# Attention followed by a two-layer gelu network on one NeuronCore: reordering attention against layer 2, and narrower filler matmuls

## The chip, the cores and the metric

The kernel runs on one core of a Trainium2 chip. A core has five engines that each work through their own instruction list: TensorE (PE in the profile, with its weight loads as PEld), VectorE (DVE), ScalarE (ACT), GpSimd (POOL) and SyncE (SP), which here only issues transfers. They meet through semaphores. The metric is the device time of one execution in microseconds; the figure that counts is the median over runs.

## The reference

Inputs are q, k and v of shape (8, 8, 576, 64): 8 batches, 8 heads, 576 tokens, 64 values per head. A third input s (8, 8, 576) makes a decay bias. For each batch and head:

```
scores = (q @ k.T) / 8
cum    = cumsum(max(s, 0))
bias   = -(cum[i] - cum[j])
scores = where(j > i, -1e9, scores + min(bias, 0))
attn   = exp(scores - max);  attn = attn / (sum(attn) + 1e-9)
out    = attn @ v
```

The heads of a token are put side by side, which gives x with 8 * 576 = 4608 rows of 512. Then `h = x @ w_in` (512 by 2048), `g = gelu(h)`, and `y = g @ w_out` (2048 by 512). The result is y, 4608 by 512 in float32.

## The kernel before, in words

Attention goes batch by batch, and within a batch by head pairs p = 0 to 3. The network goes by chunks c = 0 to 8 of 512 tokens. Batch nb = c + 1 is computed while chunk c is in its second layer, so that the matmuls of layer 2 stand between the pieces of attention. The order on each engine is the order in which the Python code issues the work (a manual schedule); a buffer pool and the semaphores it places add the waits.

The pieces are helpers:

- `tr_item(b, p, i)` (line 353) transposes q or k of a pair with 18 small matmuls and one copy (line 364). It is used for batches 0 and 1; later batches are transposed by DMA.
- `sc_item(b, p)` (line 370) makes the scores of a pair in two units of 1024 columns: ten matmuls into the PSUM tile sc_ps (line 376), and for each unit one exponential on ScalarE into P (line 392). Then `mask_item` (line 398) multiplies the triangular blocks of P by a 0/1 mask on VectorE (lines 401 and 406): one operation after the first unit, two after the second.
- `av_item(b, p)` (line 452) multiplies P with the values (avn) and with the decay weights alone (avd, the denominator): eight matmuls each (line 414). The first four of avn read unit 0 of P, the next four read unit 1. Eight short matmuls into avr follow, for the last 64 tokens. `norm` then forms 1/avd on ScalarE as a logarithm in two parts (line 431) and an exponential (line 432), and VectorE multiplies avn with it into xT (line 447).
- `l1_item(c, f2)` (line 482) is a piece of layer 1: matmuls into h_ps (line 495), gelu on ScalarE into gT (lines 501 and 504).
- `l2_item(c, sub, f0, f1)` (line 506) is part of one output tile of 128 tokens: one matmul of 512 columns for each f from f0 to f1, of 16 in all, into o_ps (line 514). After the last, VectorE copies the tile to o_sb (line 521) and SyncE writes it out (line 523).

PSUM is split by tag: "sc" has two large buffers (scores, h_ps), "mlp" one (o_ps), "av" three (avn, avd, avr, tr_ps, some o_ps).

For chunks c = 1 to 6 the second layer is a cluster that the loop at line 688 writes. Before the loop stand a quarter of output tile 0, the scores of pair 0, and the rest of output tile 0. Then for p = 1, 2, 3:

```
sc_item(nb, p)
av_item(nb, p - 1)
l2_item(c, p, 0, 12)
...                      # p = 3: av_item(nb, 3), norm_rest(nb)
l2_item(c, p, 12)
```

Chunk 0 has an order of its own, written out call by call from line 630. The prologue (lines 553 to 604) loads the first inputs, transposes batch 0 and makes its scores; `keep_busy(n)` (line 559) issues n matmuls of a zero tile into a scratch PSUM tile called warm, which nothing reads. They stand at lines 564 (eight), 568 (three), 571 (one) and 583 (one).

Of the kernel before, what the change touches and what calls it, by code (L numbers as in the profile page):

```python
# [19 lines left out]
def kernel(  # L20
# [10 lines left out]
    nc = tc.nc  # L31
# [92 lines left out]
    busy = const.tile([128, 512], bf16, name="busy")  # L124
# [67 lines left out]
    def transpose_rows(b, p):  # L192
        for i in range(2):
            nc.sync.dma_start_transpose(out=qkT[b % 2][:, i, p, :S], in_=rows_of[b, i][p % 2, p // 2])
# [175 lines left out]
    def sc_item(b, p, neg=False, masks=True):  # L370
        P_of[b, p] = P = work.tile([128, 2, PW], bf16, tag="P", bufs=4, name="P")
        for u in range(NU):
            s_ps = ps.tile([128, 2, 512], fp32, tag="sc", bufs=2, name="sc_ps")
            for jt, i0, n, off in UNITS[u]:
                for e in range(2):
                    nc.tensor.matmul(  # L376
                        s_ps[:, e, off : off + n],
                        lhsT=qkT[b % 2][e * 64 : e * 64 + 64, 1, p, jt * 128 : jt * 128 + 128],
                        rhs=qkT[b % 2][e * 64 : e * 64 + 64, 0, p, i0 : i0 + n],
                        start=True, stop=not neg, skip_group_check=neg,  # L380
                    )
            for lo, n, w in ((0, 2, 128), (448, 1, 64))[: u + 1 if neg else 0]:
                for e in range(2):
                    nc.tensor.matmul(  # L384
                        s_ps[:, e, 0:512].rearrange("p (g c) -> p g c", c=256)[:, :, 0:128]
                        if n == 2 else s_ps[:, e, lo : lo + w],
                        lhsT=ident_bf,
                        rhs=neg_bf[:, :w].unsqueeze(1).to_broadcast([128, n, w])
                        if n == 2 else neg_bf[:, :w],
                        start=False, stop=True, skip_group_check=True,  # L390
                    )
            nc.scalar.activation(  # L392
                P[:, :, UO[u] : UO[u] + UW[u]], s_ps[:, :, : UW[u]], func=AF.Exp, scale=scale
            )
            if masks and not neg:
                mask_item(b, p, u, nc.vector)
# [109 lines left out]
    def l2_item(c, sub, f0=0, f1=FT, av=False):  # L506

        gT = gT_of[c]
        if f0 == 0:
            tag, bufs = ("av", 3) if av else ("mlp", 1)  # L510
            o_of[c, sub] = ps.tile([128, KO * 128], fp32, tag=tag, bufs=bufs, name="o_ps")
        o_ps = o_of[c, sub]
        for ft in range(f0, f1):
            nc.tensor.matmul(  # L514
                o_ps, lhsT=gT[:, ft, sub * 128 : (sub + 1) * 128], rhs=w_out_r[:, ft, :],
                start=(ft == 0), stop=(ft == FT - 1),
            )
        if f1 < FT:
            return
        o_sb = work.tile([128, KO * 128], fp32, tag="osb", bufs=3, name="o_sb")  # L520
        nc.vector.tensor_copy(o_sb, o_ps)  # L521
        r0 = c * NB + sub * 128
        nc.sync.dma_start(out=out[r0 : r0 + 128, :], in_=o_sb)
# [32 lines left out]
    load_v(0, (ST - 1,))  # L556
    warm = ps.tile([128, 512], fp32, tag="mlp", bufs=1, name="warm")

    def keep_busy(n):
        for _ in range(n):  # L560
            nc.tensor.matmul(warm, lhsT=busy[:, :128], rhs=busy, start=True, stop=True)  # L561

    weights_scan()
    keep_busy(8)
    tr_item(0, 0, 0, nc.scalar.copy)
    tr_item(0, 0, 1)
    weights_dve()
    keep_busy(3)
    sc_item(0, 0, masks=False)
    tr_item(0, 1, 0)  # L570
    keep_busy(1)
    tr_item(0, 1, 1)
    nc.vector.tensor_scalar(neg_bf, tri_bf, 2048.0, -2048.0, op0=MULT, op1=ALU.add)
    weights_pe()
# [31 lines left out]
    for c in range(NCH):  # L606
        nb = c + 1
        for k0, k1 in ((0, 2), (2, 3)) if c == 0 else ((0, 3),):
            l1_item(c, 0, k0, k1)
            l1_item(c, 1, k0, k1)  # L610
        l1_item(c, 0, KO - 1)
        l1_item(c, 1, KO - 1)
        l1_item(c, 2, av=True)
        if 0 < c and nb < B:
            scale_v(nb, STS, nc.vector)
            absmax_v(nb)
        if c == 0:
            absmax_v(0)
            scale_v(0, STS[ST - 1 :], nc.vector)
        if c < B:  # L620
            for p in range(NP):
                absmax(c, p)
        if 1 < c and nb + 1 < B:
            nc.gpsimd.tensor_copy(pace, gT_of[c][:, 0, 0:1])
            load_v(nb + 1)
            if nb + 2 < B:
                load_qk(nb + 2)
        for f2 in range(3, FT // 2):
            l1_item(c, f2)
        if c == 0:  # L630
            exp_set()
            load_v(2)
            for p in range(NP):
                av_rest(0, p)
            tr_item(1, 0, 0)
            tr_item(1, 0, 1)
            l2_item(c, 0, 0, 8)
            tr_item(1, 1, 0)
            tr_item(1, 1, 1)
            norm_rest(0)  # L640
            sc_item(1, 0)
            l2_item(c, 0, 8)
            sc_item(1, 1)
            l2_item(c, 1, 0, 8, av=True)
            tr_item(1, 2, 0)
            tr_item(1, 2, 1)
            l2_item(c, 1, 8, av=True)
            tr_item(1, 3, 0)
            tr_item(1, 3, 1)
            scale_pair(1, 0)  # L650
            sc_item(1, 2)
            l2_item(c, 2, 0, 8)
            scale_pair(1, 1)
            sc_item(1, 3)
            l2_item(c, 2, 8)
            scale_pair(1, 2)
            av_item(1, 0, rest=False)
            scale_pair(1, 3)
            av_item(1, 1, wide=True, rest=False)
            l2_item(c, 3, 0, 8)  # L660
            interleave(2, "q")
            write_rows(2, 0, nc.sync)
            av_item(1, 2, wide=True, rest=False)
            l2_item(c, 3, 8)
            interleave(2, "k")
            write_rows(2, 1, nc.sync)
            av_item(1, 3, rest=False)
            for p in (0, 1):
                transpose_rows(2, p)
            gelu_set()  # L670
            for p in (2, 3):
                transpose_rows(2, p)
            nc.gpsimd.tensor_copy(pace, qkT[0][:, 1, 3, 0:1])
            load_qk(3)
            load_v(3)
            absmax_v(1)
        elif nb < B:
            exp_set()
            l2_item(c, 0, 0, 4)
            if c == 1:  # L680
                for p in range(NP):
                    av_rest(1, p)
            sc_item(nb, 0)
            if c == 1:
                norm_rest(1)
            l2_item(c, 0, 4)
            late = int(c == 1)
            for p in range(1, NP):
                if nb + 1 < B and p == 1 + late:
                    interleave(nb + 1, "q")  # L690
                    write_rows(nb + 1, 0, nc.sync)
                if nb + 1 < B and p > 1 and not late:
                    transpose_rows(nb + 1, p - 2)
                sc_item(nb, p)
                av_item(nb, p - 1)
                l2_item(c, p, 0, 12)
                if p == NP - 1:
                    if nb + 1 < B:
                        for pt in range(0 if late else p - 1, NP):
                            transpose_rows(nb + 1, pt)  # L700
                    if c == 1:
                        nc.gpsimd.tensor_copy(pace, qkT[(nb + 1) % 2][:, 1, p, 0:1])
                        load_qk(nb + 2)
                    av_item(nb, p)
                    norm_rest(nb)
                    gelu_set()
                l2_item(c, p, 12)
                if nb == B - 1 and p == 1:
                    cert_decay()
                if nb + 1 < B and p == 1 + late:  # L710
                    interleave(nb + 1, "k")
                    write_rows(nb + 1, 1, nc.sync)
        else:
            if c == B - 1:
                cert_1()
            for sub in range(4):
                if c == NCH - 1 and sub == 3:
                    l2_last(c, sub)
                    break
                l2_item(c, sub, av=sub % 2 == 0)  # L720
                if c == B - 1 and sub < 3:
                    (cert_2, cert_3, cert_4)[sub]()
# [4 lines left out]
    with tc.If(rv > 0):  # L727
        with tc.tile_pool(name="gen", bufs=1) as gen, tc.tile_pool(
# [21 lines left out]
            with tc.For_i(0, B, 1) as b:  # L750
# [8 lines left out]
                for h in range(H):  # L759
# [17 lines left out]
                    for it in range(ST):  # L777
                        n_i = 128 if it < ST - 1 else SL
                        w = min(S, (it + 1) * 128)
                        s_ps = gps.tile([128, 1024], fp32, tag="g2", bufs=2, name="gs_ps")  # L780
                        for j0 in range(0, w, 512):
# [3 lines left out]
                                rhs=tT["k"][:, j0:j1], start=True, stop=True,  # L785
# [20 lines left out]
                        for jt in range(it + 1):  # L806
# [9 lines left out]
                                lhsT=raw["v"][:n_j, jt, h0 : h0 + 2, :].rearrange("p h d -> p (h d)"),  # L816
# [57 lines left out]
```

## Time and profile before

| | us |
|---|---|
| median of 14 runs (lowest 330.61, highest 333.95) | 331.34 |
| the profiled execution, its own device time | 334.05 |
| span from its first to its last instruction | 332.3 |
| TensorE busy in the span | 320.9 (97%) |
| ScalarE busy | 203.3 (61%) |
| VectorE busy | 193.4 (58%) |
| GpSimd busy | 65.6 (20%) |

Busy time counts a matmul from its start until its result is written, so that matmuls in a stream overlap in the record: one of 512 columns has a mean of 380 ns in the profile, while the next one starts about 216 ns after it. The spacing of the starts, not the length of the records, tells how fast TensorE goes. Where a view merges several instructions, the number after x is their count; a few matmul records are missing from the trace.

### The profile page before, as it was taken

The page shows a single profiled execution, that of the slowest core. Times are in us where ns is not written, and L with a number is a line of the kernel's source. Part 1 is how long each engine was busy: PE and PEld are TensorE (multiplying, and loading weights), DVE is VectorE, ACT ScalarE, POOL GpSimd, SP SyncE. Part 2 cuts the span into 40 slices and gives each one's busy share as a digit, 9 for nine tenths or more (in the row PEclk, how much of TensorE's full clock was granted, in tenths as well). Part 3 has the DMA queues.
Part 4 walks back from the last instruction along what each step waited for, and adds up shares of the span by engine and source line. Part 5 has one row for each costly group of instructions (what it writes and reads, how often), then busy time and mean ns, then how long its engine had stood idle before and what let it go on. Part 6 is the DMA issues. An engine that isn't in the chain of part 4 may idle for free.

```text
span 332.3 us, 6357 instructions
## 1 busy us (share of the span) xinstructions
PE 320.9 (97%) x2540; PEld 165.8 (50%) x2585; DVE 193.4 (58%) x384; ACT 203.3 (61%) x288; POOL 65.6 (20%) x100
## 2 busy tenths in 40 slices
PE   8989999999999999999999999999999999999992
PEld 3664555545554455445544554455445544444452
DVE  5559468896569464947495657745693654150021
ACT  3588756669576776777576767677659566204400
POOL 8753352005200730520044002200000000000000
PEclk9999999999999999999999999999999999999999
DMA  7999999765985899999769765625600110010012
GB/s 115 220 209 209 212 198 273 237 91 89 237 253 109 149 245 278 184 137 201 225 145 234 180 179 132 142 105 174 132 4 34 45 53 0 34 63 32 3 63 71
DMA packets 53828, 47.30 MB, mean 142 GB/s; under 512 B 31328, under 2 KB 43872, under 8 KB 53792
## 3 DMA queue, kind: packets, MB, share of 16 engines
q0 software_dynamic: 15936, 23.07, 39.1%
q1 hardware_dynamic: 37856, 23.75, 27.1%
q8 instruction: 22, 0.36, 0.5%
q14 instruction: 14, 0.11, 0.1%
HBM read 36.85 MB, written 16.52 MB: 161 GB/s over the span
## 4 chain that ended last, share of the span: by engine, by line
PE 95%; DVE 1%; issue 1%; ACT 1%
PE h_ps L495 37%; PE o_ps L514 37%; PE sc_ps L376 6%; PE avn L414 4%; PE avd L414 3%; PE tr_ps L359 2%; PE warm L561 2%; PE avr L414 1%; PE o_ps L533 1%; PE avw L414 1%; PE sc_ps L384 1%; DVE qkT L364 0%; ACT ln L432 0%; ACT ln L431 0%; DVE vv L230 0%
## 5 line engine op out<-in xcount | busy, mean ns | idle before, releaser
L514 PE MATMUL o_ps<-w_out_r,gT 128*128 128x512 bf16 x533 | 127.3, 380 | 1.7 <-issue 0.5
L495 PE MATMUL h_ps<-xT,w_in_r 128*128 128x512 bf16 x560 | 125.2, 379 | 1.4 <-DVE xT L447 0.6
L495 PEld LDWEIGHTS <-w_in_r 128*128 128x128 bf16 x576 | 56.2, 98 | 68.6 <-issue 1.0
L501 ACT ACTIVATE gT<-h_ps 128x1024 bf16<-128x1024 f32 x54 | 54.3, 1023 | 49.4 <-PE h_ps L495 49.4
L392 ACT ACTIVATE P<-sc_ps 128x1024 bf16<-128x1024 f32 x64 | 62.4, 1021 | 34.9 <-PE sc_ps L376 31.8
L514 PEld LDWEIGHTS <-gT 128*128 128x128 bf16 x560 | 51.5, 98 | 59.1
L521 DVE COPY o_sb<-o_ps 128x512 f32<-128x512 f32 x35 | 24.1, 688 | 47.8 <-PE o_ps L514 47.8
L401 DVE TENSOR_TENSOR P<-P,tri_bf 128x512 bf16<-128x512 bf16 x58 | 24.1, 423 | 38.5 <-ACT P L392 38.3
L213 DVE TENSOR_REDUCE amx<-qkT 128x2 f32<-128x1152 bf16 x32 | 40.9, 1336 | 0.0
L447 DVE SCALAR_TENSOR_TENSOR xT<-avn,ln 128x256 bf16<-128x256 f32 (+3 forms) x64 | 21.7, 386 | 25.7 <-ACT ln L432 25.6
L202 POOL DMA_DIRECT2D raw_v<-in_v_dram x40 | 34.4, 880 | 8.7 <-DMA w_out_r<-in_moe_w_out_dram 4.3
L431 ACT ACTIVATE ln<-avd 128x256 f32<-128x256 f32 x56 | 18.5, 390 | 12.4 <-PE avd L414 11.0
L230 DVE TENSOR_TENSOR vv<-raw_v,wb 128x512 bf16<-128x512 f32 (+3 forms) x44 | 25.2, 632 | 0.0
L432 ACT ACTIVATE ln<-ln 128x512 f32<-128x512 f32 (+1 forms) x40 | 23.5, 587 | 1.3
L504 ACT ACTIVATE gT<-h_ps 128x512 bf16<-128x512 f32 x36 | 19.6, 602 | 6.3 <-PE h_ps L495 6.3
L376 PE MATMUL sc_ps<-qkT 64*128 64x256 bf16 (+2 forms) x320 | 22.7, 264 | 0.4 <-DVE vv L230 0.4
L220 DVE TENSOR_REDUCE amv<-raw_v 128x1 f32<-128x2048 f32 (+1 forms) x16 | 22.9, 1470 | 0.0
L376 PEld LDWEIGHTS <-qkT 64*128 64x128 bf16 x320 | 13.4, 97 | 15.4 <-issue 12.2
L414 PEld LDWEIGHTS <-vv 128*64 128x64 bf16 x384 | 17.0, 110 | 6.8 <-issue 4.2
L414 PEld LDWEIGHTS <-wb 128*64 128x64 bf16 x384 | 17.1, 111 | 0.0
L364 DVE COPY qkT<-tr_ps 128x576 bf16<-128x576 bf16 x14 | 10.2, 754 | 10.3 <-PE tr_ps L359 10.3
L414 PE MATMUL avn<-P,vv 128*64 128x256 bf16 x224 | 16.1, 265 | 0.0
(94 smaller groups left out, 168.3 us busy)
## 6 DMA issues: line engine op xcount, KB each, us to landing
out_dram<-o_sb SPq DMA_DIRECT2D x35, 256.0 KB, 2.3
raw_v<-in_v_dram POOLq DMA_DIRECT2D x32, 256.0 KB, 7.8
rows<-qk_bf SPq DMA_DIRECT2D x12, 576.0 KB, 4.7
early_q<-in_q_dram POOLq DMA_DIRECT2D x14, 288.0 KB, 10.1
early_k<-in_k_dram POOLq DMA_DIRECT2D x14, 288.0 KB, 10.4
w_in_r<-in_moe_w_in_dram POOLq DMA_DIRECT2D x4, 512.0 KB, 11.2
w_out_r<-in_moe_w_out_dram POOLq DMA_DIRECT2D x4, 512.0 KB, 14.9
raw_v<-in_v_dram POOLq DMA_DIRECT2D x8, 128.0 KB, 9.8
```

What stands on the lines that cost most here:

```text
L202: nc.gpsimd.dma_start(out=t[:n_st, st, :, :], in_=bass.AP(tensor=v.tensor, offset=v.offset + b * H * S * D + st * 128 * D, ap=[[D, n_st], ...
L213: nc.vector.tensor_reduce(amx[:, b * NP + p], qkT[b % 2][:, :, p, :S], axis=AX, op=ALU.max, apply_absolute_value=True)
L230: eng.tensor_tensor(vb[:n_st, st0:st1, h0:h1, :], t[:n_st, st0:st1, h0:h1, :], wb[:n_st, st0:st1, b * H + h0 : b * H + h1] .unsqueeze(3).t ...
L376: nc.tensor.matmul(s_ps[:, e, off : off + n], lhsT=qkT[b % 2][e * 64 : e * 64 + 64, 1, p, jt * 128 : jt * 128 + 128], rhs=qkT[b % 2][e * 6 ...
L392: nc.scalar.activation(P[:, :, UO[u] : UO[u] + UW[u]], s_ps[:, :, : UW[u]], func=AF.Exp, scale=scale)
L401: eng.tensor_tensor(d, d, tri_bf.unsqueeze(1).unsqueeze(1).to_broadcast([128, 2, 2, 128]), op=MULT)
L414: nc.tensor.matmul(out[e * 64 : e * 64 + 64, lo : lo + n], lhsT=(wb[:, jt, b * H + h : b * H + h + 1].to_broadcast([128, 64]) if den else ...
L432: nc.scalar.activation(ln[:, :w], ln[:, :w], func=AF.Exp, scale=-1.0)
L495: nc.tensor.matmul(h_of[c, f2][i], lhsT=w_in_r[:, ko, ft * 128 : (ft + 1) * 128], rhs=xT[:, ko, c * NB % XW : c * NB % XW + NB], start=(ko ...
L501: nc.scalar.activation(gT_of[c][:, f2 * 2 : f2 * 2 + 2, :], hh_of[c, f2], func=AF.Gelu)
L514: nc.tensor.matmul(o_ps, lhsT=gT[:, ft, sub * 128 : (sub + 1) * 128], rhs=w_out_r[:, ft, :], start=(ft == 0), stop=(ft == FT - 1),)
L521: nc.vector.tensor_copy(o_sb, o_ps)
```

## The change

Three edits, in different stages:

1. In the clusters of chunks 1 to 6, `av_item(nb, p - 1)` is called ahead of `sc_item(nb, p)`.
2. In chunk 0, the first half of output tile 1 comes ahead of the second half of output tile 0, so that both tiles are open at once, with the scores of pair 1 between them.
3. In the prologue, the three filler matmuls ahead of the first scores, and the one between the transposes of pair 1, have 256 columns instead of 512. The other fillers keep their width.

```diff
-    def keep_busy(n):
+    def keep_busy(n, w=512):
         for _ in range(n):
-            nc.tensor.matmul(warm, lhsT=busy[:, :128], rhs=busy, start=True, stop=True)
+            nc.tensor.matmul(warm[:, :w], lhsT=busy[:, :128], rhs=busy[:, :w], start=True, stop=True)
 
     weights_scan()
     keep_busy(8)
     tr_item(0, 0, 0, nc.scalar.copy)
     tr_item(0, 0, 1)
     weights_dve()
-    keep_busy(3)
+    keep_busy(3, 256)
     sc_item(0, 0, masks=False)
     tr_item(0, 1, 0)
-    keep_busy(1)
+    keep_busy(1, 256)
     tr_item(0, 1, 1)
...
             norm_rest(0)
             sc_item(1, 0)
+            l2_item(c, 1, 0, 8, av=True)
+            sc_item(1, 1)
             l2_item(c, 0, 8)
-            sc_item(1, 1)
-            l2_item(c, 1, 0, 8, av=True)
             tr_item(1, 2, 0)
             tr_item(1, 2, 1)
             l2_item(c, 1, 8, av=True)
...
+                av_item(nb, p - 1)
                 sc_item(nb, p)
-                av_item(nb, p - 1)
                 l2_item(c, p, 0, 12)
```

## The prediction

> **What bounds the kernel now.** I read the busy table first, then the chain of work that ended last, then the timeline of the stages that the change touches.
>
> ```profile
> PE 320.9 (97%) x2540; PEld 165.8 (50%) x2585; DVE 193.4 (58%) x384; ACT 203.3 (61%) x288; POOL 65.6 (20%) x100
> ```
>
> TensorE is busy nearly all the time, but only the spacing of matmuls says whether it loses any. The chain in the cluster of chunk 3, in order of time (start, length, what):
>
> ```profile
> 150.06 0.56 PE sc_ps L376 x10
> 150.62 0.50 PE avn L414 x8
> 151.12 0.38 PE avd L414 x8
> 151.51 0.12 PE avr L414 x8
> ...
> 155.19 0.55 PE sc_ps L376 x10
> 155.74 0.50 PE avn L414 x8
> ...
> 160.31 0.55 PE sc_ps L376 x10
> 160.85 0.50 PE avn L414 x8
> ```
>
> From one pair's scores to the next takes 5.13 and 5.12 us. The work alone: scores 0.55, the three av groups 1.01 (0.50 + 0.38 + 0.12 and rounding), 16 matmuls of output about 3.56. That is 5.12. So the clusters have no wait on TensorE that a reorder could remove. Any gain there is zero; what the reorder may add is the question. For that, the timeline of ScalarE and VectorE (start, length, what, count, idle before):
>
> ```profile
> 148.23 1.94 ACT L392 ACTIVATE P<-sc_ps 128x1024 bf16<-128x1024 f32 x2
> 150.21 0.42 DVE L401 TENSOR_TENSOR P<-P,tri_bf 128x512 bf16<-128x512 bf16 x1 [0.49 <-ACT P L392]
> 150.55 0.57 PE L414 MATMUL avn<-P,vv 128*64 128x256 bf16 x8
> 150.96 0.55 PE L414 MATMUL avd<-P,wb 128*64 128x256 bf16 x8
> ...
> 157.38 0.67 ACT L431 ACTIVATE ln<-avd 128x256 f32<-128x256 f32 x2
> 158.08 0.63 ACT L432 ACTIVATE ln<-ln 128x512 f32<-128x512 f32 x1
> ```
>
> The second mask of pair 0 ends at 150.63. Today av(0) follows the scores of pair 1 and starts at 150.55, with its second half at about 150.79: just in time. The prologue:
>
> ```profile
> 6.01 1.46 PE L561 MATMUL warm<-busy 128*128 128x512 bf16 x3
> 7.41 1.03 PE L376 MATMUL sc_ps<-qkT 64*128 64x256 bf16 x10
> ```
>
> Three fillers run up to the first scores, about 0.43 us apart.
>
> **What the Trainium skill says.** "TensorE: Matmul & The Clock Gate", Part 1 (The HAM clock gate): TensorE starts at half clock and is released after a window of about 3.4 us of activity; the window runs freely, so the release varies from run to run; matmuls of 512 start every 426.7 ns before it and 215.7 ns after. The trace agrees: 427 ns between fillers, 216 ns in layer 2, with half-rate spacing until about 20.7 us here. The same page, Part 3 (The mechanism): matmuls are strict FIFO. A matmul that waits therefore holds up all behind it. Its Part 1 (Architectural detail) says that ScalarE and VectorE are strict FIFO too; the trace agrees: avd of the second pair shown is done at 156.62, but L431 starts at 157.38, behind exponentials issued before it.
>
> **The change part by part.**
>
> *Clusters, p = 1.* av(0) now starts where the scores of pair 1 started: 150.00 (chunk 3). Its first four matmuls read unit 0, masked long ago; with eight avn in 0.41 us and the last pair half as wide they take 0.24. The fifth waits for the second mask, 150.63, plus about 0.05 for the handover (L447 ends 24.83, its matmul starts 24.88): 150.68 instead of 150.24, a wait of 0.44. Queued behind it on TensorE: the rest of av(0), the scores of pair 1, the output tile. The same rows in chunks 2, 4, 5 and 6 (boundary and mask end: 115.44 and 116.07; 184.56 and 185.19; 219.11 and 219.74; 253.67 and 254.30) give 0.44 each. In chunk 1 avr of the batch before puts 0.6 us of matmuls ahead, the mask ends at 81.06 against a start at 80.89, and avn does not wait. But avr takes the third "av" buffer, freed by L447 at 81.79; it would start at 81.68 and waits 0.15. Sum: 5 x 0.44 + 0.15 = 2.35.
>
> *Clusters, p = 2 and 3.* The order on ScalarE changes: logarithms and exponential of av(p-1) now stand ahead of the exponentials of pair p. From the start of av(p-1): avd done 0.96, handover 0.04, L431 to L432 0.70, L432 0.63, two exponentials 1.94, handover 0.04, second mask 0.42, handover 0.05, in all 4.78. TensorE comes to the fifth avn of the next av after 1.01 + 0.55 + 3.56 + 0.24 = 5.36 at p = 2 and at av(2): covered by 0.58. VectorE fits in between: L447 (0.76) runs while ScalarE makes unit 0, and the interleave (0.82) is done by then. For av(3) only 12 output matmuls (2.70) lie between: 1.01 + 0.55 + 2.70 + 0.24 = 4.50. The fifth avn waits 4.78 - 4.50 = 0.28. Six clusters: 1.7. What follows (reciprocal, gelu table, layer 1) moves along with TensorE and keeps its distances. SyncE's and GpSimd's orders are unchanged; the change of PSUM users adds no type switch: three per round before and after, about 0.1 each, inside the sums above.
>
> Clusters in all: 2.35 + 1.7 = about 4.05 lost. If the cover at p = 2 is gone as well, another 0.3 per boundary for twelve boundaries would be 3.6.
>
> *Chunk 0.* The first half of tile 1 starts at 42.98 in the place of the second half of tile 0 and takes an "av" buffer whose copy (L364) runs 42.26 to 43.02: it waits 0.04 to 0.1. The copy of tile 0 (0.69) moves behind the masks of pair 1 and ahead of two transposes' copies (0.75 each), which end at 49.9; the transposes that need those buffers come at 49.71 (its buffer free at 49.2) and 49.98, the scores at 50.40. Hidden with 0.1 to 0.5 left; at worst 0.2. Tile 0's transfer out (SyncE, L523, first of two at 46.03) is issued some 2.5 later, still the first in SyncE's list; its o_sb is not reused before 61.66. w_out's last part lands at about 40.9 (issued 24.3, 16.6 to landing), used at 43.9 before: nothing waited, so later use saves nothing. I take +0.05.
>
> *Fillers.* In the profiled execution three fillers at 0.213 instead of 0.427 end 0.64 earlier, but the scores need the copy of k (6.12 + 0.76 = 6.88): start 6.93 instead of 7.41, 0.48 gained. The single one gains 0.21: the transposes behind it start right after it, and k of pair 1 has landed at 8.45 (3.15 + 5.3). Values (last at 16.3) and w_in (first at 18.9) arrive in time for work 0.69 earlier. Gain 0.69; if the release of the clock stays at 20.7, av(0) of batch 0 runs longer at half rate and 0.2 comes back: 0.5 to 0.7. Where the clock is released early, the fillers hide nothing on the path: k of pair 0 lands at 5.37, transposes and copy make the scores start at about 6.6 whatever the fillers do, and pair 1's k lands after a short filler would end. There the gain is 0.
>
> **Sum.** In the profiled execution 4.05 + 0.05 - 0.6 = +3.5 on 334.05. That execution is 2.7 above the median, and ten of 14 runs lie within 330.6 to 331.7. I read this as the prologue's late clock release, which the median run would not have (an inference; the trace shows one release). For the median I take 4.1 less 0.2 for the fillers: 331.34 + 3.9 = 335.2.
>
> **Rivals.**
> 1. *Only the p = 1 waits appear.* The chain to av(3) is a sum of eight terms against a cover 0.28 short; ScalarE gaps 0.05 smaller each would close it. Then 331.34 + 2.35 + 0.05 - 0.2 = 333.5. For it: the margin is small. Against: ScalarE's rows repeat to 0.01.
> 2. *The clock is released later.* Shorter fillers are less activity. If typical runs turn into ones like the profiled, 2.7 comes on top, less the 0.6: 331.34 + 4.1 + 2.7 - 0.6 = 337.5. Against: what is removed is 0.85 us of activity, and real matmuls move up.
> 3. *Not slower: the masks come in time.* If gelu, table load and exponentials of pair 0 end 0.44 earlier against TensorE than traced, as in chunk 1, and by the same shift the last masks come 0.28 earlier, no wait arises: 331.34 + 0.05 - 0.6 = 330.8. It decides at those 0.44 and 0.28. Against: ScalarE has no idle time from the last gelu to pair 0's exponentials in five clusters, and four of them agree to 0.01.
> 4. *The cover at p = 2 runs out too* (VectorE's interleave waiting for its load, as once at 117.57): up to 339; with half of it 337.
>
> **How the numbers follow.** Sum as worked out 0.70; only p = 1 0.10; late clock 0.09; cover gone 0.06; masks in time 0.05. Time 335.2, the likeliest case alone 334.5 to 335.9. For 8 in 10 the range runs from 333.9 to 337.2: most of the first case, part of the second, and part of the cases above. 0.3% is 1.0 us, about what a measurement of this kernel can tell from no change. Only the third rival can bring it below 330.35 or inside the bound, so slower 0.94, same 0.03, faster 0.03.
>
> **What would show it.** Right: in chunks 2 to 6 waits of TensorE on VectorE's L401 of about 0.4 inside the av group at p = 1 and 0.3 at av(3), rounds of 5.1 us at p = 2, clusters 0.7 longer in chunks 2 to 6; first scores near 6.9 with half-rate spacing. Wrong: clusters of the old length (rival 3), or waits at p = 2. The forecast falls if the second mask is ahead of the fifth avn matmul, or if the start of layer 1 loses a wait that the trace of before hides.

## The result, and the profile after

The changed kernel takes 336.21 us (median of 10 runs, 334.87 to 337.14) against 331.70 for the kernel before in the runs beside it (47 runs, 330.61 to 334.81). The ratio, which is not the quotient of the two medians, is 1.0126, with an interval of 1.0102 to 1.0150: about 4.2 us slower, 3.4 to 5.0. The forecast was 335.2 us, in a range of 333.9 to 337.2. The profiled execution after took 337.13 us with a span of 335.3; the one before had 334.05 and 332.3.

The busy table of the page after, and the shares of the chain of work that ended last by engine, from the same page:

```profile
PE 322.9 (96%) x2541; PEld 166.2 (50%) x2585; DVE 194.8 (58%) x384; ACT 203.1 (61%) x288; POOL 65.3 (19%) x100
...
PE 86%; ACT 6%; issue 3%; DVE 2%; DMA 1%; POOL 0%; POOLq 0%
```

The busy table hardly moved. The chain did: before, TensorE held 95% of it and ScalarE 1%. Now ScalarE has 6% and VectorE 2%, so the end is set in part by work on those engines. The chain in the cluster of chunk 3 shows where (start, length, what):

```profile
149.03 1.95 ACT P L392 x2
...
151.00 0.43 DVE P L401
151.44 0.04 issue
151.48 0.36 PE avn L414 x4
...
152.34 0.55 PE sc_ps L376 x10
...
157.46 0.55 PE sc_ps L376 x10
...
162.57 0.55 PE sc_ps L376 x10
```

The chain leaves TensorE ahead of p = 1: exponentials of pair 0, second mask, then the last four avn matmuls. From one pair's scores to the next it is 5.12 and 5.11 us, as before, so p = 2 waits for nothing. The list of TensorE's waits (waiting tile, what it waited for, us in total, times, longest) has one entry in the clusters that was not there before:

```profile
PE avn L414 <- DVE P L401: 1.4, 5, 0.3
```

Five times, once in each of chunks 2 to 6, as forecast. The record counts only the idle time after a matmul's modelled end, so 0.3 each is too little: the fifth avn in chunk 3 starts at 151.48. Without a wait it starts 0.24 after the first (150.79), which would be 151.03, so the wait is 0.45. A second wait doesn't show in that list at all. It stands in the timeline of the changed kernel at av(3) (start, length, engine, line and operation, count, idle before):

```profile
163.18 0.63 ACT L432 ACTIVATE ln<-ln 128x512 f32<-128x512 f32 x1
163.72 1.92 ACT L392 ACTIVATE P<-sc_ps 128x1024 bf16<-128x1024 f32 x2
...
165.67 0.42 DVE L401 TENSOR_TENSOR P<-P,tri_bf 128x512 bf16<-128x512 bf16 x1 [0.49 <-ACT P L392]
165.75 0.76 PE L414 MATMUL avn<-P,vv 128*64 128x256 bf16 x8
```

The group avn takes 0.76, and its second half starts at 166.15, once the mask has ended at 166.09. In the kernel before, the same group had its full speed:

```profile
164.49 0.57 PE L414 MATMUL avn<-P,vv 128*64 128x256 bf16 x8
```

That is 0.16 to 0.19 of waiting, hidden inside the length of a merged row.

The prologue of the changed kernel, in the same columns:

```profile
6.24 0.82 PE L561 MATMUL warm<-busy 128*128 128x256 bf16 x3
7.17 1.03 PE L376 MATMUL sc_ps<-qkT 64*128 64x256 bf16 x10
```

The first scores start 0.24 earlier (7.17 against 7.41). They would have started earlier still, but k of pair 0 landed later: its transposes start at 5.62 against 5.39.

Where the time went is best read from the starts of layer 1 (the first matmul into h_ps of each chunk). The table gives these for all profiled executions of this study: when TensorE's clock was released to its full rate, the start of layer 1 in chunk 0, then the length of each chunk from that start to the next, and the start of the last matmul into o_ps. All in us, from rounded starts, so that the last digit can be off by one; labels are those of the sections below. The release comes early in some executions and late in others, whichever kernel it is; this is taken up below.

| kernel | release | layer 1 | chunk 0 | chunk 1 | chunk 2 | mean of 3 to 6 | last matmul |
|---|---|---|---|---|---|---|---|
| before | 20.76 | 23.91 | 38.33 | 35.03 | 34.55 | 34.56 | 325.88 |
| after | 20.64 | 23.47 | 38.56 | 35.39 | 35.20 | 35.20 | 329.25 |
| before, once more | 4.42 | 20.10 | 40.70 | 35.02 | 34.56 | 34.55 | 324.44 |
| after, once more | 4.02 | 19.38 | 39.85 | 36.47 | 35.20 | 35.20 | 327.54 |
| e1_clusters | 5.30 | 19.80 | 39.86 | 35.63 | 35.30 | 35.36 | 327.85 |
| e2_chunk0 | 5.11 | 19.99 | 39.66 | 35.02 | 34.61 | 34.56 | 323.34 |
| e3_fillers | 20.62 | 23.37 | 38.49 | 35.02 | 34.56 | 34.55 | 325.50 |
| e4_norm_behind | 4.63 | 20.30 | 40.00 | 36.32 | 35.82 | 35.84 | 331.63 |
| e6_no_mask | 6.48 | 19.95 | 40.52 | 35.84 | 34.75 | 34.79 | 326.04 |
| e7_p1_only | 9.82 | 20.70 | 39.57 | 35.30 | 35.19 | 35.01 | 326.65 |
| e8_p23_only | 5.46 | 19.91 | 42.70 | 35.20 | 34.74 | 34.74 | 327.34 |
| e9_no_fillers | 4.72 | 22.27 | 38.32 | 35.03 | 34.55 | 34.56 | 324.23 |
| e10_2and3 | 20.35 | 23.30 | 38.51 | 35.02 | 34.56 | 34.56 | 325.45 |
| e11_k_first | 4.56 | 19.32 | 40.54 | 35.02 | 34.56 | 34.56 | 323.50 |

Between the first two rows, chunks 2 to 6 give 5 x 0.64, chunk 1 gives 0.36, and prologue and chunk 0 together give back 0.21. The sum is 3.4, and the last matmul starts 3.37 later.

### The profile page after: what moved, and what is told of

Read it like the earlier page. It is cut to its first block, busy times and chain, and to the rows that moved or that the text cites. A ratio compares the mean times of both kernels' runs of the same rounds, so it can differ in the third digit from the quotient of the medians.

```text
span 335.3 us, 6340 instructions
## 1 busy us (share of the span) xinstructions
PE 322.9 (96%) x2541; PEld 166.2 (50%) x2585; DVE 194.8 (58%) x384; ACT 203.1 (61%) x288; POOL 65.3 (19%) x100
## 4 chain that ended last, share of the span: by engine, by line
PE 86%; ACT 6%; issue 3%; DVE 2%; DMA 1%; POOL 0%; POOLq 0%
PE h_ps L495 37%; PE o_ps L514 32%; PE sc_ps L376 5%; PE avn L414 4%; PE avd L414 3%; ACT P L392 3%; PE tr_ps L359 2%; ACT gT L504 2%; PE avr L414 1%; DMA early_k<-in_k_dram 1%; PE o_ps L533 1%; PE avw L414 1%; DVE P L401 1%; ACT L541 1%; PE sc_ps L384 1%
## 5 line engine op out<-in xcount | busy, mean ns | idle before, releaser
L431 ACT ACTIVATE ln<-avd 128x256 f32<-128x256 f32 x56 | 18.4, 380 | 40.4 <-PE avd L414 39.0
L213 DVE TENSOR_REDUCE amx<-qkT 128x2 f32<-128x1152 bf16 x32 | 40.9, 1336 | 0.0
L432 ACT ACTIVATE ln<-ln 128x512 f32<-128x512 f32 (+1 forms) x40 | 23.5, 588 | 1.3
L414 PE MATMUL avn<-P,vv 128*64 128x256 bf16 x224 | 18.1, 266 | 1.4 <-DVE P L401 1.4
L414 PEld LDWEIGHTS <-wb 128*64 128x64 bf16 x384 | 17.8, 111 | 0.0
L414 PE MATMUL avd<-P,wb 128*64 128x256 bf16 x224 | 15.7, 259 | 0.0
```

The lines of the kernel that those rows point to most:

```text
L213: nc.vector.tensor_reduce(amx[:, b * NP + p], qkT[b % 2][:, :, p, :S], axis=AX, op=ALU.max, apply_absolute_value=True)
L414: nc.tensor.matmul(out[e * 64 : e * 64 + 64, lo : lo + n], lhsT=(wb[:, jt, b * H + h : b * H + h + 1].to_broadcast([128, 64]) if den else ...
```

## The experiments

**Each edit alone.** Three kernels with one edit each.

```diff
# e1_clusters
-                sc_item(nb, p)
                 av_item(nb, p - 1)
+                sc_item(nb, p)
# e2_chunk0
             sc_item(1, 0)
+            l2_item(c, 1, 0, 8, av=True)
+            sc_item(1, 1)
             l2_item(c, 0, 8)
-            sc_item(1, 1)
-            l2_item(c, 1, 0, 8, av=True)
# e3_fillers
-    keep_busy(3)
+    keep_busy(3, 256)
...
-    keep_busy(1)
+    keep_busy(1, 256)
```

> Only the cluster edit. Theory (a mask or a chain of ScalarE is late for the earlier av matmuls): nearly the whole of the change, TensorE's end 3.6 us later in the profile than before (0.64 in each of chunks 2 to 6, 0.36 in chunk 1), time 3.4 to 4.2 us above before. Rival (a later clock release through the fillers makes a good part of it): 2.5 us or less.

Measured: 335.83 us (19 runs) against 331.82, ratio 1.0116 (1.0091 to 1.0141). The waits for the mask are there five times, 1.4 us, as in the changed kernel. The one edit carries nearly the whole loss. In chunk 3 a transpose by DMA came 0.6 late, once (sc_ps waited), which is why its mean is above 35.20.

> Only the edit of chunk 0. Theory: 0.05 to 0.1 us lost at the start of output tile 1, which waits for a transpose's copy; no change that the times can tell (within 0.3 us). Rival (it gives back time where w_out or a copy was late): faster by 0.2 us or more.

Measured: 331.72 us (20 runs) against 331.82, ratio 0.9974 (0.9951 to 0.9996). The medians agree to 0.1. The interval of the ratio leaves out 1, which speaks for the rival; but the times fall into two groups (see the next run), and within the lower one, below 332.95, the medians here and before are both 331.6. What differs is that 2 of 20 times lie above, where before it were 20 of 58. Whether the edit does that or chance does is not shown, so at most it is a small gain. Its trace differs from the first one of before already in the prologue, which the edit does not touch: the clock was released at 5.11 instead of 20.76.

> Only the narrower fillers. Theory: where the clock is released late, as in the profiled executions, 0.3 to 0.7 us faster; where early, no change; the share of late ones as before; median 0 to 0.3 us below before. Rival (less activity means later releases): more of the times in the upper group 2 to 3 us above the lower one, median above before by 0.3 us or more.

Measured: 332.58 us (22 runs) against 331.82, ratio 1.0003 (0.9983 to 1.0023). In its trace the scores start at 6.99 and the last matmul 0.38 earlier than before. But the times fall into two groups, before and with this edit. Before: 38 times below 332.95 with a median of 331.57, and 20 above with 333.84. With the edit: 12 below with 332.05, and 10 above with 333.28. The upper group gained 0.5 and the lower lost 0.5. The trace is of an execution of the upper group (333.35). For the lower group there is none with this edit alone, but the mean clock that was granted to each execution splits it: five with 0.995 took 331.29 to 331.82, seven with 0.981 to 0.987 took 332.02 to 332.67. The lower group lost its 0.5 in executions in which the clock was taken back for a time; the trace of e9_no_fillers (below) shows what such a mean stands for.

**Which wait: p = 1 or p = 2 and 3.** Edit 1 was made for one boundary, and for the other two.

```diff
# e7_p1_only
-                sc_item(nb, p)
-                av_item(nb, p - 1)
+                if p == 1:
+                    av_item(nb, p - 1)
+                    sc_item(nb, p)
+                else:
+                    sc_item(nb, p)
+                    av_item(nb, p - 1)
# e8_p23_only: the same with p > 1 in place of p == 1
```

> The cluster edit at p = 1 alone, p = 2 and 3 as before. Theory: chunks 2 to 6 each 0.46 us longer in the profile, chunk 1 by 0.18: 2.5 us in all. Rival (the two waits are one that moves on): 3.6 us as with the whole cluster edit.

Measured: 334.24 us (19 runs) against 332.41 on that chip, ratio 1.0058 (1.0037 to 1.0079), and chunks 3 to 6 at 35.01, that is 0.46 each above 34.55. Chunk 1 lost 0.28 and chunk 2 0.64, more than expected; in chunk 2 VectorE's interleave waited 2.81 for its load, and the masks of pair 1 stood behind it. TensorE's waits:

```profile
PE avn L414 <- DVE P L401: 1.4, 5, 0.3
```

> The cluster edit at p = 2 and 3 alone, p = 1 as before. Theory: a wait of 0.17 us at av(3) in each of chunks 1 to 6, none at p = 2: 1.0 us in all. Rival (the two waits are one that moves on): nothing, or 3.6 us.

Measured: 333.12 us (11 runs; a twelfth took 337.95), ratio 1.0015 (0.9989 to 1.0042). Chunks 2 to 6 take 34.74, 0.18 each above 34.55, and chunk 1 0.17 above 35.03. TensorE doesn't appear as waiting for a mask; again only the length of the group at av(3) tells, where it was 0.57 before:

```profile
165.22 0.76 PE L414 MATMUL avn<-P,vv 128*64 128x256 bf16 x8
```

So 0.46 and 0.18 add up to the 0.64 per chunk of the changed kernel, and nothing of it is at p = 2. The time of the traced execution (335.20) overstates the loss in the clusters: chunk 0 took 42.70 there, for a reason of its own (below).

**Is it the mask?** With edit 1, the second mask of pair 0 is not applied in the clusters.

```diff
# e6_no_mask: edit 1, and
-            if masks and not neg:
+            if masks and not neg and not (b > 1 and p == 0 and u == 1):
```

> The cluster edit alone, and the masks of unit 1 of pair 0 left out in the clusters (that part of the scores stays unmasked; all else is computed). Theory (the wait at p = 1 is for that mask and nothing else): no wait inside the av group at p = 1; chunks 2 to 6 each 0.15 to 0.2 us longer than before (the wait at av(3) alone), where the cluster edit made 0.64. Rival (the exponential of unit 1 itself, or the order of matmuls): 0.4 or more stays.

Measured: one time, 334.28 us, with chunk 2 at 34.75 and chunks 3 to 6 at 34.79 in the mean. Of 0.64 lost per chunk 0.2 is left, the part at av(3). (In chunk 3 av(3) did not wait, but o_ps did, 0.30 for a copy to o_sb.) The avn group at p = 1 has its full speed, here in chunk 3:

```profile
149.23 0.58 PE L414 MATMUL avn<-P,vv 128*64 128x256 bf16 x8
```

The mask was what p = 1 waited for.

**Can the loss be moved off ScalarE?** If only the matmuls of av go first, and its logarithms, exponential and multiply stay behind the exponentials and masks of the next pair, the chain to av(3) loses its 1.2 us of logarithms and exponential (0.70 and 0.54).

```diff
# e4_norm_behind
-    def av_item(b, p, wide=False, rest=True, last=False):
+    def av_item(b, p, wide=False, rest=True, last=False, later=False):
...
+        if later:
+            return num, den
         norm(b, p, p + 1, num, den, 0, CUT, [(0, 0, 256), (1, 256, CUT)])
...
+                nd = av_item(nb, p - 1, later=True)
                 sc_item(nb, p)
-                av_item(nb, p - 1)
+                norm(nb, p - 1, p, *nd, 0, CUT, [(0, 0, 256), (1, 256, CUT)])
```

> The cluster edit alone, with the av matmuls ahead of the scores on TensorE, but the logarithms, the exponential and the multiply of the norm behind the scores' exponentials and masks, as in the kernel before. Theory (the wait at av(3) comes from ScalarE taking the norm first): that wait is gone, the one of 0.44 at p = 1 stays; TensorE's end 2.2 to 2.6 us later than before. Rival (the wait at av(3) comes from the matmuls' order itself): as with the cluster edit alone, 3.6 us.

Measured: 339.35 us (4 runs), ratio 1.0212 (1.0154 to 1.0269). Neither forecast came true. The wait for the mask at av(3) is indeed gone (avn takes 0.57 again), but another took its place. The timeline of this kernel in chunk 3, at av(3):

```profile
165.57 0.57 PE L414 MATMUL avn<-P,vv 128*64 128x256 bf16 x8
...
165.95 0.76 DVE L447 SCALAR_TENSOR_TENSOR xT<-avn,ln 128x256 bf16<-128x256 f32 x2 [0.65 <-ACT ln L432]
166.76 0.57 PE L414 MATMUL avd<-P,wb 128*64 128x256 bf16 x8 [0.62 <-DVE xT L447]
```

avd of the last pair needs an "av" buffer, and the multiply of the pair before, which frees it, is now late. Three buffers allow one av in flight and no more. Its matmuls start 1.19 after those of avn (166.76 less 165.57) instead of 0.41: 0.78 lost, beside the 0.46 at p = 1, which stayed. Chunks 3 to 6 are 1.28 longer than before. A variant with only the multiply behind would meet the same buffer, and was not run.

**The two groups of times.** There is a second trace of each of the kernels before and after, and one of a kernel without the four narrowed fillers.

```diff
# e9_no_fillers
-    keep_busy(3)
...
-    keep_busy(1)
```

> The kernel before without the four fillers that the change narrows. Theory (fillers cost time only where the clock is released late): executions with a late release about 0.5 us faster than those of before, the others the same. Rival (the fillers buy early releases): clearly more executions in the upper group than the third of before, median 0.5 us or more above.

Measured: 332.60 us (20 runs) against 332.41, ratio 0.9994 (0.9974 to 1.0014). The fillers that the change narrows are worth nothing to the median, and 8 of 20 times lie above 332.95 where 17 of 46 did. The windows of this trace show that they still do something (stretch, its length, PE, PEld, DVE, ACT, POOL busy with counts, clock, DMA share, GB/s):

```profile
4.00:8.00 4.00, 2.68 (x66) 1.48 (x64) 3.15 (x5) 1.89 (x4) 4.00 (x8) 1.00 1.10 162
8.00:12.00 4.00, 3.90 (x55) 2.46 (x56) 2.04 (x4) 2.22 (x5) 4.00 (x6) 0.52 1.11 221
```

The clock was released at 4.72 (the view counts what lies ahead of the first recorded change as full) and taken back at 8.14, after TensorE had stood idle for 0.86 and 0.48 us, and stayed at half until 18.38. Layer 1 starts at 22.27 instead of about 20. And yet the execution took 332.16, as long as others: chunk 0 took 38.32 instead of 39.6 to 40.7, and no matmul in it waits for w_out.

The mean clock of this execution, 0.982, is the mark of such a loss: 10.24 us at half the clock are 0.016 of the span, and the last 1.4 us, again at half, 0.002. It lets the executions without a trace be counted. A mean below 0.985 stands in none of the 137 executions of the kernel before that ran beside these experiments and in none of the 74 of e1, e2, e4, e7 and e8, which have the wide fillers; it stands in 10 of 20 without the narrowed fillers, and in 15 of 68 with narrow ones (3 of the 12 of the changed kernel whose clock is on record, 5 of 22 of e3_fillers, 1 of 13 of e10_2and3, 6 of 21 of e11_k_first, the last two below). So the fillers do buy something where the release is early: they keep the clock. That the loss falls in the prologue is seen in the trace of e9_no_fillers alone; for the narrow fillers there is only the mean.

> The kernel before once more, for its trace. If the clock is released at about 5 us: layer 1 starts at 19.8 to 20.3 instead of 23.9, chunk 0 waits 1.1 to 2.5 for the last part of w_out, span 329.5 to 330.8. If it is released at about 20.7: as the first trace, span 332.3.

Measured: one time, 332.50 us, clock released at 4.42. TensorE's waits in it begin with:

```profile
PE o_ps L514 <- DMA w_out_r<-in_moe_w_out_dram: 2.1, 1, 2.1
```

Layer 1 starts 3.8 earlier than in the first trace of the same kernel, and 2.4 of it is lost again in chunk 0, most of it in this one wait.

> The changed kernel once more, for its trace. Released at about 5 us: layer 1 starts at about 20, no wait for w_out but 0.9 for k of batch 1 in chunk 0, clusters as in its first trace (chunks 2 to 6 at 35.2), span 333 to 333.8. Released at about 20.7: span 335.3.

Measured: one time, 335.44 us, clock released at 4.02. The clusters of chunks 2 to 6 are as in the first trace (35.20). In chunk 0 no matmul waits for w_out, but the transposes of k of batch 1 wait 1.0. And chunk 1 takes 36.47, 1.1 more than in the first trace. Its timeline:

```profile
87.32 0.83 DVE L178 COPY qk_bf<-early_q 128x1152 bf16<-128x1152 bf16 x2 [3.34 <-DMA early_q<-in_q_dram]
...
89.27 0.69 PE L414 MATMUL avn<-P,vv 128*64 128x256 bf16 x8 [0.90 <-DVE P L401]
```

VectorE's interleave of q for batch 3 waits 3.34 for its load. Behind it stand the multiply (88.07) and only then the masks of pair 2 (88.80), and av(2) waits 0.90 for those. In the second trace of the kernel before, the same interleave starts later still (88.18, after waiting 2.82), and yet chunk 1 takes 35.02: there the masks come right behind it (88.93 to 89.82), the multiply after them, and av(2) starts at 90.22, behind the scores of pair 3. So edit 1 brings av(2) 0.55 forward and puts the multiply's 0.73 ahead of its masks, a swing of 1.3 where before there were 0.4 to spare (that TensorE ran 1.6 later there moves both). In e1, e6 and e8, which also reorder p = 2 and 3, chunk 1 took 35.63, 35.84 and 35.20 with an early release; with the old order in the clusters it took 35.02 or 35.03 in all seven traces.

**A version that beats both?** The edits without the clusters, and the same with k of batch 1 loaded and transposed earlier, so that chunk 0 should wait less.

```diff
# e10_2and3: edits 2 and 3
# e11_k_first: edits 2 and 3, and
-    for i in range(4):
+    for i in range(3):
         load_w(1, i)
     for n in "qk":
         load_early(1, n, 2)
+    load_w(1, 3)
...
-            l2_item(c, 0, 8)
             tr_item(1, 2, 0)
             tr_item(1, 2, 1)
+            l2_item(c, 0, 8)
```

> The kernel before with the changed order of chunk 0 and the narrower fillers, the clusters left as they were. Theory (the whole loss sits in the clusters): within 0.3% of the kernel before, 331 to 332 us, clusters of chunks 2 to 6 at 34.55 per chunk, no wait of avn for a mask. Rival (the edits act on each other, chunk 0 with narrower fillers loses something of its own): over 333.

Measured: 332.72 us (13 runs) against 331.73, ratio 1.0020 (0.9995 to 1.0044), clusters at 34.56. The loss is in the clusters; the other two edits are no gain either.

> As the run above, with q and k of the second pairs of batch 1 issued ahead of the last part of w_out, and their transposes ahead of the second half of tile 0. Theory (where the clock is released at about 5 us, chunk 0 waits for its transfers, 0.9 to 1.3 in the traces so far): that wait goes, chunk 0 takes 38.4 to 38.9 instead of 39.7 there, and the median falls by 0.5 to 1.0, to about 330.8. Rival (the queue delivers at its rate, and whatever comes last is waited for): another tile is waited for, the median within 0.3% of the run above.

Measured: 332.53 us (21 runs) against 331.73, ratio 1.0006 (0.9986 to 1.0025). The rival held. From the waits of this kernel:

```profile
PE o_ps L514 <- DMA w_out_r<-in_moe_w_out_dram: 1.1, 1, 1.1
```

k is no longer waited for, w_out is again, and chunk 0 takes 40.54. The queue moves some 205 GB/s from 30 to 38 us, and what it brings last is waited for. Seven of the 21 executions have a mean clock of 0.979 to 0.986; the same order with the wide fillers was not run. No version faster than the kernel before was found.

## Why the prediction was right, and where it was not

**What bounds the kernel: right.** The clusters had no wait to remove; rounds at p = 2 kept their 5.1 us, and what edit 1 did there was only to add.

**p = 1: right in place and size.** 0.44 was forecast for chunks 2 to 6, and 0.46 measured in chunks 3 to 6 with this boundary alone; without the mask it vanishes. In chunk 1 the wait of avr for its buffer was put at 0.15, and the changed kernel shows 0.18.

**av(3): right in place, the size was off.** The step "0.70, L432 0.63, two exponentials 1.94" gave 4.78 against a cover of 4.50, a wait of 0.28. Measured: 0.18. The term that was mis-sized is the one from L432 to the first exponential. The timeline of av(3) above has it: L432 starts at 163.18 and is 0.63 long, but the exponential behind it starts at 163.72, after 0.54. The forecast added the lengths of records where an engine overlaps its instructions; it used the spacing for L431 (0.70 for two rows of 0.38) and not for L432. With 0.54, and 1.92 for the exponentials, the chain is 4.67 and the wait 0.17. The Trainium skill has the number, on the page "ScalarE: Activation LUTs", section "What ACT_TABLE_LOAD costs": activations back to back overlap by about 93 ns. The trace agrees, 0.63 less 0.54; the prediction did not use it. The traces before and after add a condition: L432 reads what L431 has just written, and there it never overlaps but starts 0.03 after L431's end, in all 40 places of each. Six clusters make 1.1 instead of 1.7, and the clusters about 3.6 instead of 4.05.

**Chunk 0: right for the profiled execution, the reason incomplete.** Forecast +0.05. e10 against e3 gives 38.51 against 38.49. (Between the first two rows of the table chunk 0 is 0.23 longer: 0.16 is a wait of layer 1, see the fillers, and 0.1 the expected wait at the start of tile 1.) But the step "w_out's last part lands at about 40.9, used at 43.9 before: nothing waited" holds only where the clock comes late. In the second trace of before, layer 1 starts 3.8 earlier, and w_out is late by 2.06. There the new order takes that wait away and puts another (0.9 to 1.0, for k of batch 1) in its place. In the times no gain from this is seen within the lower group (e2_chunk0).

**Fillers: half right.** For a late release 0.5 to 0.7 was forecast. With the edit alone the scores start 0.42 earlier and layer 1 0.54; at the last matmul 0.38 is left, since layer 1 then waits 0.16 longer for xT (0.74 against 0.58). In the changed kernel k landed 0.23 later, and less was gained. For an early release the forecast was 0, "whatever the fillers do", and this step was wrong. It asked only whether the fillers stand on the path of the first scores, not whether the clock stays released behind them. With narrow fillers it was taken back in about a fifth of the executions (15 of 68, by their mean clock), before in none of 137; in the lower group of e3_fillers the medians with and without such a loss are 332.19 and 331.38.

**The rivals.** "Only the p = 1 waits appear" (333.5): no, av(3) waits as well, though by little. "Masks in time" (330.8): no. "Clock released later": before and after each had one early and one late release among their two traces, and a change in their share is not shown. But the reason given for this rival, less activity, was sound: what came is a clock taken back. Three of the 12 executions of the changed kernel have a mean of 0.980 to 0.982 and took 336.08 to 337.01; the four shortest, at 0.998, took 334.87 to 335.80. "The cover at p = 2 runs out", with VectorE's interleave waiting for its load, came true in some executions: in chunk 1 with an early release, where the masks behind it came 0.90 late in the second trace of after, and in chunk 2 of e1_clusters and e7_p1_only, where av(1) lost 0.1 to 0.2.

**The sum.** For the profiled execution +3.5 was forecast; the last matmul starts 3.37 later, and the device time grew by 3.08, since the tail behind that matmul was 0.3 shorter. For the median +3.9 was forecast and about 4.2 measured (3.4 to 5.0). The clusters were overestimated by 0.5, and the fillers were put at a gain; what may make up for both is chunk 1 with an early release and the executions that lose their clock. How much each adds to the median is not settled. That the forecast of the median came as close as it did is in part luck: errors of opposite sign met.

## What to carry to other kernels

A stretch in which the bounding engine has no wait can't gain from a reordering; ask only which producers the moved consumer now runs ahead of, and count the whole chain to the last half of its operand. Make such a sum from the starts of instructions, not from their lengths, and look for small waits in the lengths of merged rows, since the list of waits can leave them out. Where transfers bound a stage, as in chunk 0 here, taking away one wait may only show the next, so a reordering is worth no more than the difference between the two. Work that hides nothing on the path may still hold the clock, so compare the granted clock of many executions before narrowing it.

## What the runs showed of the hardware that was not expected

- **The clock changes on a grid of 3.413 us that has a phase of its own in each execution.** In all 14 traces the recorded changes lie whole steps apart: in e8_p23_only 5.46, 43.01 and 46.42 (11 and 12 steps), in e9_no_fillers 4.72, 8.14 and 18.38 (1 and 4), in the others one release and one change back at the end, 90 to 97 steps later. Eight fillers fill TensorE from 1.20 to 4.6 in every trace. The release came at 4.02 to 5.46 in eight of the 14 traces, at 6.48 and 9.82 in two, and at 20.35 to 20.76 in four, whichever kernel it was. Counted back in steps of 3.413, a window ended at 4.02 to 5.46 in the first group, at 3.0 to 3.1 in the two, and at 3.3 to 3.7 in the four. So the windows that released had at least 2.8 us of fillers, or fillers and transposes, in them, and those that ended earlier had 1.8 to 2.5 and did not. This fits all 14; what decides in the windows after that one is not shown (at nearly the same phase, the two were released one and two windows later), and the phase was not varied. The Trainium skill, "TensorE: Matmul & The Clock Gate", Part 1 (The HAM clock gate), says that the window runs freely and takes about 3.4 us, but expects the release to vary by 0.5 us; here it varied by over 16.
- **A late release costs far less than it looks.** Layer 1 starts 3.8 later, the device time is only 1.6 longer (334.05 against 332.50), since with an early release chunk 0 waits for its transfers. The two groups of times of the kernel before, of which the upper has the late release in the one trace taken in it, are 2.3 apart.
- **A wait of 2.5 us was enough to lose the clock.** In e8 the wait for w_out lasted 2.48, and the windows show half the clock in the 3.4 us after it:

```profile
40.00:43.00 3.00, 0.52 (x3) 0.19 (x2) 1.05 (x4) 0.95 (x2) 0.12 (x1) 1.00 1.35 181
43.00:46.40 3.40, 3.40 (x18) 1.24 (x16) 1.12 (x2) 1.64 (x2) 1.62 (x3) 0.50 1.02 188
```

  43.01 is the release at 5.46 plus eleven windows, and the wait (40.16 to 42.64) lies inside the last of them. The wait of 2.06 in the second trace of before didn't do it: it ran from 40.35 to 42.41, across the edge of a window at 41.97, so that no window held more than 1.6 of it. The same page of the Trainium skill ("Why this matters for your kernels") warns of gaps above about 3 us; here a shorter one, inside one window, sufficed.
